# Products on half tiles, products of zeros in early gaps, and a new order of three half groups, in an attention kernel with two gated layers

## The chip, the cores and the metric

The kernel runs on one core of a Trainium2 chip. The time is the device time of one execution in microseconds (us), and a kernel is judged by the median of its runs. Engines are named as the profile names them: PE is TensorE (matrix products), DVE is VectorE, ACT is ScalarE, POOL is GpSimd, SP issues the DMA transfers. PEld is the loading of weights into PE.

## What is computed

Eight heads of linear attention with a decaying state run over four batches of 768 tokens. The 3072 tokens then go through two gated layers.

```python
# attention: B=4, H=8, S=768, D=48
for t in range(S):
    state = alpha[:, :, t, :, None] * state + einsum('bhd,bhe->bhde', k[:, :, t], v[:, :, t])
    y[:, :, t] = einsum('bhd,bhde->bhe', q[:, :, t], state)
x = y.transpose(0, 2, 1, 3).reshape(3072, 384)
# layer one: d_ff = 2048
h = x @ w_in;  x = (h * cos(h)) @ w_out
# layer two: d_ff = 1536
out = ((x @ w_a) * (x @ w_b)) @ w_out2
```

## The kernel before

**Units.** Attention is done in 48 units. A unit is 64 tokens of one batch with all 8 heads (12 units to a batch). For a unit DVE scans the decays forward (L303) and backward (L315), with a reciprocal between them (L312). `m` holds queries times forward decay and is made on POOL by two instructions of 48 partitions (L327). `k` holds keys times backward decay (L340, on DVE for units 0 to 7, on POOL after that). PE then forms the scores (L374) and the transposed keys (L383). DVE masks the scores (L407 in units 0 to 15, four instructions at L413 later), and ACT copies the keys (L389). PE next forms the new part of the state (L444, old state L450) and the outputs (L461). Units 0 to 15 have a separate product of the old state with `m` (L466, in the units that have an old state). It takes the state as one operand of 112 rows, half of which meet zeros in `m`, and each of its eight products stands behind an output product. From unit 16 on the state lies beside the values and needs no product of its own. ACT (L505) and DVE (L508) write each output as a high and a low part into the input tile `x_t` of the layers. DVE brings the state to the next unit (L535), from unit 16 on by two sums (L546) and two POOL instructions (L549).

From unit 8 on, one "block" on PE holds the outputs of a unit, the scores and transposed keys of the next unit and the new state of this one.

**Groups and steps.** 8 units (512 tokens) are a group; there are 6. Layer one is done in 96 steps (g, f): group g with slice f of the 16 slices of d_ff. A step has 9 products of 512 columns into a bank `hp` (L656), then round, fraction, sine, product and the split into two parts (ACT L706, DVE L709, ACT L714, DVE L717, ACT L721, DVE L725), then 9 products into the accumulator `acc_t` (L663). I call 9 such products a "PE group" of work. Layer two has 72 steps of 27 products (L656 and L663 again).

**Weights.** Layer one's weights arrive in 16 pairs, each 768 KB (L595). A pair is converted by ACT (L599, L604), by DVE (L610, L616), by ACT (L625) and by POOL (L636). A pair is needed from the first step of its f on.

**What sets the order.** The code does not emit instructions directly. It enters operations with an estimated duration and due time into a `Plan`, which lists them by its own rules, and each engine then runs its instructions in the listed order. `h_at` holds the due times of the steps, here group after group; `unit_due` holds those of the units. The 8 units of group 1 are due along the 16 steps of group 0, 1.7 steps apart, and so on. The order of the steps is this loop:

```python
    for g in range(NG):
        for f in range(NF1):
            h_at.append(t)
            t += TAU0 if g == 0 else TAU if g < NG - 1 else TAUL
```

**Products of zeros.** `keep_warm` issues products of zeros into accumulator bank 0 (L671): 15 at the start, one behind each of units 0 to 7. Their results are not used.

Of the kernel before, what the change touches and what calls it, by code (L numbers as in the profile page):

```python
# [57 lines left out]
NLATE = NPAIR2 - NPAIR1  # L58
DVE_DECAY = 0
ACT_LOW = 16  # L60
FIRST_UNIT, EVERY = 0.6, 1.7
PE, DVE, ACT, POOL, SP = range(5)


class Plan:
# [39 lines left out]
    def run(self):  # L105
# [56 lines left out]
        self.done = done  # L162
        return done
# [3 lines left out]
def chunked(ctx: ExitStack, tc: tile.TileContext, u_in: bass.AP, wts: bass.AP, out: bass.AP, in_range: bass.AP):  # L167
# [3 lines left out]
    xpool = ctx.enter_context(tc.tile_pool(name="xpool", bufs=2))  # L171
# [50 lines left out]
    h_at = []  # L222
    t = T0
    for g in range(NG):
        for f in range(NF1):
            h_at.append(t)
            t += TAU0 if g == 0 else TAU if g < NG - 1 else TAUL
# [39 lines left out]

    def xtile(g):
        if g not in xg:
            t = xpool.tile([P, 2, NP, G], F32R, name="x_t")  # L270
            xg[g] = t[:, 0], t[:, 1], t
        return xg[g]

    def plan_load(u):
        d, ops = un[u], U[u]
        if "ld" in ops:
            return ops["ld"]
        def load():
            if u < UG:
                t = wpool.tile([P, 2, 2 * DM], F32R, name="w_t").bitcast(F32)  # L280
                d["in"] = t.rearrange("p a c -> p (a c)")[:, 0:IN_COLS]
            else:
                d["in"] = att.tile([P, IN_COLS], F32, name="in_t", bufs=NIN)
            cols = W_A + 2 * NE4 if u < APART else IN_COLS
            cuts = (0, NA + 1, cols) if u == 0 else (0, cols)
            for c0, c1 in zip(cuts, cuts[1:]):
                nc.sync.dma_start(out=d["in"][:, c0:c1], in_=u_in[u, :, c0:c1])

        ops["ld"] = op(SP, 1.5, load, lag=1.7)
        ops["in_last"] = take("w_t", NPAIR1, ops["ld"]) if u < UG else take("in", NIN, ops["ld"])  # L290
        return ops["ld"]

    def plan_front(u):
# [20 lines left out]
        def scan_r():  # L314
# [13 lines left out]
                    m[rows, i + apart], part(u, 0)[rows], d["a"][rows, :, 1:], op=ALU.mult  # L328
# [3 lines left out]
            for rows, i in HEADS  # L332
# [29 lines left out]
    def plan_scores(u, block=None):  # L362
# [7 lines left out]
        def score():  # L370
            for c in range(2):
                for b in range(2):
                    for rows, h in HEADS:
                        nc.tensor.matmul(  # L374
                            sc_t[rows_of(b, h), b, c, :], kt[rows, 2 * b + c, :],
                            m[rows, h + apart, 2 * b + c, :], start=True, stop=True,
                        )
# [44 lines left out]
    def plan_back(u):  # L422
# [32 lines left out]
        def outputs():  # L455
            for p in range(NP):
                b, c = divmod(p, 2)
                for h, r0, n in ((0, 0, C), (1, 64, D)):
# [3 lines left out]
                        ys_t[r0:r0 + n, b, c, :], w[0:k_rows], m[0:k_rows, 0 if apart else h, p, :],  # L462
                        start=True, stop=not carry,
# [18 lines left out]
        else:  # L482
# [11 lines left out]
            us = ou = op(PE, 1.75 + (1.0 if carry else 0.0), block, [kn, ld, *mk, *ma, *before], due=due)  # L494
# [19 lines left out]
        if off == 0:  # L514
            E["xl", g] = take("x", 2, xh)
            E["xfirst", g] = xh
# [152 lines left out]
    def keep_warm(n):  # L669
        for _ in range(n):  # L670
            nc.tensor.matmul(warm[0:64, :], zeros[:, 0:64], zeros, start=True, stop=True)  # L671


    x2, x2s = {}, {}

    def plan_step(g, f):
        s = H[1, g, f] = {}
        i = g * NF1 + f
        at = h_at[i]
# [59 lines left out]
        def mm2():  # L739
            if f == 0:  # L740
                acc[g] = [acc_t[:, j] for j in range(KT)]
            into(acc[g], w1s[f, 1], s["hi"], s["lo"], f == 0, f == NF1 - 1)

        o = op(PE, 2.05, mm2, [gh, gl, H[1, g, f - 1]["o"] if f else None], due=at + 11.0)
        if g == 0 and f == 0:
            need(o, *(x for u in range(UG) for x in U[u]["read"]))
        if f == 0:
# [5 lines left out]
        if f == NF1 - 1:  # L753
            def evac(j):
                if j == 0:
                    x2[g] = (right[0] if g < NG - 2 else late[0]).tile([P, KT, G], F32, name=f"x2_{g}")
                nc.scalar.mul(x2[g][:, j, :], acc[g][j], TWO_PI / WS)

            gate = E["right"] if g < NG - 2 else E["late"]
            ev, e0 = [], None  # L760
            for j in range(KT):
                e0 = op(ACT, 0.6, lambda j=j: evac(j), [o, gate, e0])
# [5 lines left out]
    def plan_x2(g):  # L768
# [4 lines left out]
        for j in range(KT):  # L773
            def hi(j=j):
                if j == 0:
                    t = xpool.tile([P, 2, NP, G], F32R, name="x_t")
# [9 lines left out]
            if j == 0:  # L786
                E["x2l", g] = take("x", 2, h)
# [88 lines left out]
    with tc.manual_schedule():  # L876
# [44 lines left out]
        for g in range(NG):  # L921
            for f in range(NF1):
                plan_step(g, f)
# [11 lines left out]
def step_by_step(  # L935
# [76 lines left out]
    with tc.For_i(0, NG, 1) as g:  # L1012
        cols = bass.ds(g * G, G)
        x = pool.tile([P, KT, G], F32, name="g_x", bufs=1)
        for j in range(KT):
            for r0, f0, n in (
                (0, 2 * j * D, D), (48, 6 * D + j, 16), (64, (2 * j + 1) * D, D), (112, 7 * D + j, 16)
# [118 lines left out]
```

## Time and profile before

| what | us |
|---|---|
| runs of the kernel | 973.31, 973.96, 976.26 (median 973.96) |
| the profiled execution's own time | 973.26 |
| its span, first to last instruction | 971.4 |
| PE busy in the span | 939.9 (97%) |
| DVE, ACT, POOL busy | 540.5, 403.2, 226.5 |

The profile takes one execution. A busy PE is not PE at its peak: its matmuls overlap, and small products that wait on each other also count. Shares over the whole span mix stages with different limits, so the stages have to be read apart. The granted clock of PE (PEclk) is 1.00 at 2.4 GHz and 0.50 at 1.2 GHz; its mean over the span is 0.991.

### The profile page before, as it was taken

What the parts mean: (1) busy time and instruction counts of PE and PEld (TensorE: products, weight loads), DVE (VectorE), ACT (ScalarE), POOL (GpSimd) and SP (SyncE); (2) the same over time, 40 slices, a digit from 0 to 9 for tenths busy, and PEclk for the clock granted to TensorE, in tenths of its full rate; (3) what the DMA queues carried; (4) which work ended last, traced back from release to release, by engine and by line L of the source; (5) the groups of instructions that cost most, each with busy time, mean ns of one, the idle gap of its engine ahead of it and who ended that gap; (6) DMA issues with size and microseconds to landing.
All of it is one profiled execution on the core that took longest, in us unless ns stands there. A gap on an engine that the chain in (4) does not pass through costs nothing.

```text
span 971.4 us, 16849 instructions
## 1 busy us (share of the span) xinstructions
PE 939.9 (97%) x6935; PEld 766.3 (79%) x6935; DVE 540.5 (56%) x951; ACT 403.2 (42%) x754; POOL 226.5 (23%) x259
## 2 busy tenths in 40 slices
PE   6798989999999999999999999999999999999996
PEld 4677768888888888888887888888888888888884
DVE  7899998767777786776777842222222222222221
ACT  3477755545545455446665523112113113112111
POOL 4556543313322232312224321001001001000000
PEclk8999999999999999999999999999999999999998
DMA  9355412212221221203223400000000000000000
GB/s 369 106 199 184 164 38 78 90 62 81 88 63 54 89 89 54 64 1 139 98 98 112 149 0 33 1 1 33 1 0 33 1 1 33 0 1 33 1 1 36
DMA packets 17700, 64.96 MB, mean 67 GB/s; under 512 B 2384, under 2 KB 4816, under 8 KB 17616
## 3 DMA queue, kind: packets, MB, share of 16 engines
q1 hardware_dynamic: 17616, 63.81, 19.0%
q8 instruction: 56, 0.92, 0.4%
q14 instruction: 28, 0.23, 0.1%
HBM read 56.72 MB, written 4.72 MB: 63 GB/s over the span
## 4 chain that ended last, share of the span: by engine, by line
PE 87%; DVE 6%; DMA 2%; ACT 2%; issue 1%; POOL 1%; SPq 0%; ACTq 0%
PE acc_t L663 33%; PE hp L656 18%; PE xy L656 15%; PE ap L656 15%; PE xy L461 2%; DMA st_t<-wts 2%; PE xy L374 1%; DVE wf_t L610 1%; DVE wf_t L616 1%; DMA w_t<-u_in 1%; PE xy L383 1%; DVE c_t L709 1%; DVE ar_t L303 1%; PE xy L444 1%; DVE glo_t L725 1%
## 5 line engine op out<-in xcount | busy, mean ns | idle before, releaser
L663 PE MATMUL acc_t<-ghi_t,w_t 128*128 128x512 f32 x972 | 301.1, 391 | 1.0 <-ACT ghi_t L721 1.0
L656 PE MATMUL hp<-x_t,w_t 128*128 128x512 f32 (+1 forms) x882 | 216.4, 390 | 3.2 <-DMA x_t<-x_t 3.2
L663 PEld LDWEIGHTS acc_t<-ghi_t,w_t 128*128 128x128 f32 x972 | 181.6, 188 | 39.3 <-ACT ghi_t L721 1.9
L663 PE MATMUL acc_t<-glo_t,w_t 128*128 128x512 f32 x486 | 190.1, 391 | 3.8 <-DVE glo_t L725 3.8
L822 DVE TENSOR_TENSOR xy<-c_t,xy 128x512 f32<-128x512 f32 x72 | 50.1, 696 | 258.0 <-PE xy L656 257.9
L656 PEld LDWEIGHTS hp<-x_t,w_t 128*128 128x128 f32 x882 | 161.1, 188 | 36.8 <-ACT w_t L625 3.3
L656 PE MATMUL xy<-x_t,w_t 128*128 128x512 f32 x594 | 145.6, 390 | 0.0
L656 PE MATMUL ap<-x_t,w_t 128*128 128x512 f32 x540 | 132.2, 389 | 0.0
L656 PEld LDWEIGHTS xy<-x_t,w_t 128*128 128x128 f32 x594 | 111.5, 188 | 23.4
L656 PEld LDWEIGHTS ap<-x_t,w_t 128*128 128x128 f32 x540 | 101.4, 188 | 21.1
L819 ACT COPY c_t<-ap 128x512 f32<-128x512 f32 x72 | 42.3, 587 | 167.9 <-PE ap L656 167.8
L663 PEld LDWEIGHTS acc_t<-glo_t,w_t 128*128 128x128 f32 x486 | 91.2, 188 | 25.6 <-DVE glo_t L725 6.4
L826 ACT CAST ghi_t<-xy 128x512 fp32r<-128x512 f32 x72 | 42.2, 586 | 138.3 <-DVE xy L822 138.3
L706 ACT ACTIVATE c_t<-hp 128x512 int32<-128x512 f32 x96 | 57.5, 599 | 67.4 <-PE hp L656 67.1
L636 POOL TENSOR_TENSOR w_t<-wf_t,w_t 128x768 fp32r<-128x768 f32 x32 | 64.0, 1999 | 92.1 <-ACT w_t L625 92.1
L781 POOL TENSOR_TENSOR x_t<-x,x_t 128x512 fp32r<-128x512 f32 x18 | 23.7, 1343 | 251.0 <-ACT x_t L778 251.0
L714 ACT ACTIVATE c_t<-c_t 128x512 f32<-128x512 f32 x96 | 60.6, 631 | 46.7 <-DVE c_t L709 45.9
L709 DVE CUSTOM_DVE_ANT_0 c_t<-c_t,hp 128x512 f32<-128x512 int32 x96 | 65.6, 683 | 25.6 <-ACT c_t L706 24.7
L721 ACT CAST ghi_t<-hp 128x512 fp32r<-128x512 f32 x96 | 56.4, 587 | 54.1 <-DVE hp L717 53.5
L717 DVE TENSOR_TENSOR hp<-c_t,hp 128x512 f32<-128x512 f32 x96 | 65.8, 685 | 19.7 <-ACT c_t L714 19.2
L830 DVE TENSOR_TENSOR glo_t<-xy,ghi_t 128x512 fp32r<-128x512 f32 x72 | 49.8, 692 | 47.3 <-ACT ghi_t L826 47.3
L725 DVE TENSOR_TENSOR glo_t<-hp,ghi_t 128x512 fp32r<-128x512 f32 x96 | 65.7, 684 | 17.1 <-ACT ghi_t L721 16.3
(100 smaller groups left out, 923.3 us busy)
## 6 DMA issues: line engine op xcount, KB each, us to landing
st_t<-wts SPq DMA_DIRECT2D x34, 768.0 KB, 4.3
in_t<-u_in SPq DMA_DIRECT2D x32, 626.0 KB, 3.8
in_t<-u_in SPq DMA_DIRECT2D x8, 578.0 KB, 9.5
out<-o_t SPq DMA_DIRECT2D x18, 256.0 KB, 2.1
w_t<-u_in SPq DMA_DIRECT2D x7, 578.0 KB, 7.8
x_t<-x_t SPq DMA_DIRECT2D x48, 48.0 KB, 2.9
w_t<-u_in SPq DMA_DIRECT2D x1, 447.5 KB, 3.5
w_t<-u_in SPq DMA_DIRECT2D x1, 130.5 KB, 2.2
```

The costliest lines, as they stand in the source:

```text
L636: nc.gpsimd.tensor_tensor(t[:, 1], conv.pop(i), t[:, 0].bitcast(F32), op=ALU.subtract)
L656: nc.tensor.matmul(acc, wt[:, w, j * P:(j + 1) * P], r[:, j, :], start=i == 0, stop=i == len(terms) - 1)
L663: nc.tensor.matmul(accs[j], wt[:, w, j * P:(j + 1) * P], r, start=first and i == 0, stop=last and i == 2)
L706: nc.scalar.activation(s["c"].bitcast(I32), s["u"], AF.Identity, bias=-0.25, scale=-1.0)
L709: nc.vector._custom_dve(TENSOR_ADD_SAT, out=s["c"], in0=s["c"].bitcast(I32), in1=s["u"], s0=0.25, s1=-0.75)
L714: nc.scalar.activation(s["c"], s["c"], AF.Sin, bias=math.pi / 2, scale=TWO_PI)
L717: nc.vector.tensor_tensor(s["u"], s["c"], s["u"], op=ALU.mult)
L721: nc.scalar.copy(s["hi"], s["u"])
L725: nc.vector.tensor_tensor(s["lo"], s["u"], s["hi"].bitcast(F32), op=ALU.subtract)
L819: nc.scalar.copy(s["c"], s["a"])
L822: nc.vector.tensor_tensor(s["b"], s["c"], s["b"], op=ALU.mult)
L830: nc.vector.tensor_tensor(s["lo"], s["b"], s["hi"].bitcast(F32), op=ALU.subtract)
```

## The change

Three things are changed, with what they need.

1. The product of the old state works on 48 rows instead of 112. `m` of units 0 to 15 loses its zero half (two planes instead of three), its two POOL instructions become one of 112 partitions, and the eight state products of a unit stand together behind its output products. The heads of two of the four pairs swap their rows in the output, so the list of rows in the weights changes (`LOW`, `HIGH`). The loads of units 0 to 15 get 16 more columns.
2. The one product of zeros behind each of units 0 to 7 goes. In its place `filled` puts products of zeros wherever the plan sees a gap on PE before its 75th microsecond: 40 beside the 15 at the start. When the accumulator is in use they add zeros to it.
3. Layer one runs steps (0, 0..7), then (1, 0..15), then (0, 8..15), then groups 2 to 5. The accumulator of the first half of group 0 is copied out by ACT, and DVE adds the second half to it (three instructions). Units 8 to 15 are due 0.9 of a step apart along the first 8 steps. Units 16 to 23 are due 0.85 of a step apart from step 24 on, because their `x` tile is that of group 1 (`SLOT`). Layer one's first `x` tiles and `x2` of group 0 get fixed places.

```diff
+LOW, HIGH = (0, 2, 5, 7), (1, 3, 4, 6)
+F0 = 8
+STEPS = (
+    [(0, f) for f in range(F0)] + [(1, f) for f in range(NF1)] + [(0, f) for f in range(F0, NF1)]
+    + [(g, f) for g in range(2, NG) for f in range(NF1)]
+)
+SLOT = (0, 1, 1, 0, 1, 0), (1, 0, 1, 0, 1, 0)
...
-        return done
+        return self.filled(done)
+
+    WARM, WARM_UNTIL, WARM_GAP = 0.39, 75.0, 0.35
+
+    def filled(self, done):
+
+        out, end = [], None
+        for o in done:
+            if o["engine"] == PE:
+                if end is not None and o["start"] < self.WARM_UNTIL:
+                    n = int((o["start"] - end - self.WARM_GAP) / self.WARM)
+                    if n > 0:
+                        out.append(dict(o, i=-1, us=n * self.WARM, start=end, fn=lambda n=n: self.warm(n)))
+                end = o["start"] + o["us"]
+            out.append(o)
+        return out
...
-    m_t = [att.tile([P, 3, NP, C], F32, name=f"m{i}", bufs=1) for i in range(3)]
-    for i, t in enumerate(m_t):
-        (nc.gpsimd if i else nc.vector).memset(t[:, 1:3], 0.0)
+    m_t = [att.tile([P, 2, NP, C], F32, name=f"m{i}", bufs=1) for i in range(3)]
...
+        t += TAU0 if n < F0 else TAUL if n < F0 + NF1 or g == NG - 1 else TAU
...
-        i, part = divmod((u // UG - 1) * NF1 + FIRST_UNIT + EVERY * (u % UG), 1)
+        g, n = divmod(u, UG)
+        first, every = {1: (0.0, 0.9), 2: (F0 + NF1 + 0.3, 0.85)}.get(g, ((g - 1) * NF1 + FIRST_UNIT, EVERY))
+        i, part = divmod(first + every * n, 1)
...
-            for rows, i in HEADS
+            for rows, i in (((slice(0, 112), 1),) if apart else HEADS)
...
-                    if carry:
-                        nc.tensor.matmul(
-                            ys_t[r0:r0 + D, b, c, :], s_t[u % 2][:, p * D:p * D + D], m[0:112, h + 1, p, :],
-                            start=False, stop=True,
-                        )
-            if u < UG:
-                keep_warm(1)
+            if carry:
+                for c in range(2):
+                    for b in range(2):
+                        for rows, h in HEADS:
+                            p, r0 = 2 * b + c, rows_of(b, h).start
+                            nc.tensor.matmul(
+                                ys_t[r0:r0 + D, b, c, :], s_t[u % 2][rows, p * D:p * D + D], m[rows, 1, p, :],
+                                start=False, stop=c == 1,
+                            )
...
-        if f == NF1 - 1:
+        if ends:
...
+                if g == 0 and f == NF1 - 1:
+                    nc.vector.scalar_tensor_tensor(
+                        x2[g][:, j, :], acc[g][j], TWO_PI / WS, x2[g][:, j, :], op0=ALU.mult, op1=ALU.add
+                    )
+                else:
+                    nc.scalar.mul(x2[g][:, j, :], acc[g][j], TWO_PI / WS)
...
-        for g in range(NG):
-            for f in range(NF1):
-                plan_step(g, f)
+        for g, f in STEPS:
+            plan_step(g, f)
```

The order of instructions that the plan makes of this is seen at three places. In the changed file lines are numbered anew: L486 is the output product (before L461), L495 the state product (L466), L467 and L473 the new and old state (L444, L450), L397 and L406 scores and transposed keys (L374, L383), L698 zeros (L671), L683 and L690 the layers' products (L656, L663). On DVE L326 and L338 are the scans (L303, L315), L335 the reciprocal (L312), L637 and L643 the weights' bits (L610, L616), L430 the mask (L407), L562 the state (L535), L535 the output's low part (L508), L739, L747 and L755 a step's fraction, product and low part (L709, L717, L725).

PE, unit 2 at the end of its new state, before:

```order
L450 MATMUL xy<-s_105,ident 112x96 x2
L461 MATMUL xy<-m_101,w_t 64x64
L466 MATMUL xy<-m_101,s_105 48x64
L461 MATMUL xy<-m_101,w_t 48x64
L466 MATMUL xy<-m_101,s_105 48x64
```

Three more such fours follow, then one product of zeros. The same place after the change:

```order
L473 MATMUL xy<-s_102,ident 112x96 x2
L486 MATMUL xy<-m_101,w_t 64x64
L486 MATMUL xy<-m_101,w_t 48x64
L486 MATMUL xy<-m_101,w_t 64x64
L486 MATMUL xy<-m_101,w_t 48x64 x2
L486 MATMUL xy<-m_101,w_t 64x64
L486 MATMUL xy<-m_101,w_t 48x64
L486 MATMUL xy<-m_101,w_t 64x64
L495 MATMUL xy<-m_101,s_102 48x64 x8
L397 MATMUL acc_t<-m_99,k_105 64x64 x8
L406 MATMUL acc_t<-ident,k_105 64x48 x8
```

The state products moved behind the outputs, and the zeros moved behind the next unit's transposed keys.

DVE, from the first step's low part to the second step's product, before (`m_99` is here the mask of unit 9; unit 10's comes later):

```order
L315 SCALAR_TENSOR_TENSOR ar_t<-in_t,last 112x260
L725 TENSOR_TENSOR glo_t<-hp,ghi_t 128x512
L610 SCALAR_TENSOR_TENSOR wf_t<-wf_t,st_t 128x768
L535 TENSOR_TENSOR s_106<-xy,ar_t 112x192
L407 TENSOR_TENSOR m_99<-xy,mask 128x256
L508 SCALAR_TENSOR_TENSOR x_t<-xy,x_t 112x4x64
L709 ISA c_t<-c_t,hp 128x512
L616 SCALAR_TENSOR_TENSOR wf_t<-st_t,wf_t 128x768
L717 TENSOR_TENSOR hp<-c_t,hp 128x512
L303 SCALAR_TENSOR_TENSOR ar_t<-in_t,first 112x260
L610 SCALAR_TENSOR_TENSOR wf_t<-wf_t,st_t 128x768
```

And after, from the first step's fraction to the second's:

```order
L739 ISA c_t<-c_t,hp 128x512
L338 SCALAR_TENSOR_TENSOR ar_t<-in_t,last 112x260
L562 TENSOR_TENSOR s_103<-xy,ar_t 112x192
L430 TENSOR_TENSOR m_99<-xy,mask 128x256
L535 SCALAR_TENSOR_TENSOR x_119<-xy,x_119 112x4x64
L747 TENSOR_TENSOR hp<-c_t,hp 128x512
L637 SCALAR_TENSOR_TENSOR wf_t<-wf_t,st_t 128x768
L643 SCALAR_TENSOR_TENSOR wf_t<-st_t,wf_t 128x768
L755 TENSOR_TENSOR glo_t<-hp,ghi_t 128x512
L326 SCALAR_TENSOR_TENSOR ar_t<-in_t,first 112x260
L562 TENSOR_TENSOR s_102<-xy,ar_t 112x192
L430 TENSOR_TENSOR m_100<-xy,mask 128x256
```

The units of group 1 moved forward: unit 10's mask (to `m_100`) now stands ahead of the second step's fraction. Counted over the whole list ahead of the 16th step's fraction, DVE has 20 forward scans, 19 backward scans and 16 weight pairs before, and 18, 18 and 15 after; the masks of units 0 to 15 and 15 earlier steps are ahead of it in both.

PE, steps 24 and 25 after the change, with the blocks of units 17 and 18:

```order
L486 MATMUL xy<-m_101,in_t 64x64
L397 MATMUL xy<-m_99,k_104 64x64 x8
L406 MATMUL xy<-ident,k_104 64x48 x8
L467 MATMUL xy<-in_t,kn_107 48x48 x8
L683 MATMUL hp<-x_118,w_t 128x512 x9
L690 MATMUL acc_t<-ghi_t,w_t 128x512 x2
L690 MATMUL acc_t<-glo_t,w_t 128x512
L690 MATMUL acc_t<-ghi_t,w_t 128x512 x2
L690 MATMUL acc_t<-glo_t,w_t 128x512
L690 MATMUL acc_t<-ghi_t,w_t 128x512 x2
L690 MATMUL acc_t<-glo_t,w_t 128x512
L486 MATMUL xy<-m_99,in_t 64x64
```

Two or three PE groups stand between blocks there, two in all cases but one, through units 16 to 23; before, two to four stood between the same units, four in most cases. No block stands between unit 15's and unit 16's, and unit 16's comes behind the first products of step (1, 15).

## Rows read from the trace of the kernel before

**Rows 1.** Windows: length, busy us of PE, PEld, DVE, ACT, POOL; clock, DMA, GB/s.

```profile
12.60:19.43 6.83, 5.04 (x85) 4.12 (x85) 3.57 (x10) 1.30 (x3) 2.98 (x4) 0.50 1.03 419
...
37.60:125.00 87.40, 76.79 (x951) 62.08 (x944) 82.00 (x117) 63.20 (x115) 54.91 (x42) 0.98 0.50 171
125.00:139.00 14.00, 12.88 (x56) 10.03 (x55) 13.72 (x25) 6.49 (x12) 5.98 (x7) 1.00 0.06 16
139.00:450.00 311.00, 311.00 (x3070) 252.19 (x3069) 231.49 (x496) 158.25 (x328) 90.56 (x149) 1.00 0.22 72
450.00:962.00 512.00, 511.71 (x2250) 421.74 (x2248) 185.44 (x254) 158.09 (x262) 58.45 (x35) 1.00 0.09 31
```

**Rows 2.** Timeline of PE in layer two: start, duration, instruction (PE groups).

```profile
898.52 2.21 PE L656 MATMUL ap<-x_t,w_t 128*128 128x512 f32 x9
900.56 2.20 PE L656 MATMUL xy<-x_t,w_t 128*128 128x512 f32 x9
```

**Rows 3.** Timeline of PE: units 1 and 2, from new state to next scores.

```profile
14.30 0.68 PE L444 MATMUL acc_t<-w_t,kn 64*48 64x48 f32 x16 [2.27 <-DVE m L407]
...
18.23 0.70 PE L374 MATMUL xy<-m,k 48*64 48x64 f32 x16
...
20.57 0.45 PE L444 MATMUL xy<-w_t,kn 64*48 64x48 f32 x16 [1.23 <-DVE m L407]
...
22.79 0.46 PE L374 MATMUL acc_t<-m,k 48*64 48x64 f32 x16
```

**Rows 4.** Timeline of DVE: masks of units 1 and 7.

```profile
13.86 0.39 DVE L407 TENSOR_TENSOR m<-acc_t,mask 128x256 f32<-128x256 f32 x1
...
38.16 0.42 DVE L407 TENSOR_TENSOR m<-acc_t,mask 128x256 f32<-128x256 f32 x1 [0.42 <-ACT kn L389]
```

**Rows 5.** Timeline at 52 us: POOL and a DVE instruction on weights.

```profile
52.67 0.68 POOL L327 TENSOR_TENSOR m<-in_t,ar_t 48x256 f32<-48x256 f32 x1
52.71 3.28 DVE L610 SCALAR_TENSOR_TENSOR wf_t<-wf_t,st_t 128x768 int32<-128x768 int32 x1
...
53.31 1.86 POOL L636 TENSOR_TENSOR w_t<-wf_t,w_t 128x768 fp32r<-128x768 f32 x1
```

**Rows 6.** Groups by form, 37.6 to 125 us: count, busy us, mean ns, idle before.

```profile
L327 POOL TENSOR_TENSOR m<-in_t,ar_t 48x256 f32<-48x256 f32 x18 | 17.6, 977 | 4.0 <-DVE ar_t L303 3.2
...
L610 DVE SCALAR_TENSOR_TENSOR wf_t<-wf_t,st_t 128x768 int32<-128x768 int32 x14 | 20.0, 1429 | 0.1
L616 DVE SCALAR_TENSOR_TENSOR wf_t<-st_t,wf_t 128x768 int32<-128x768 int32 x14 | 16.3, 1165 | 0.0
L303 DVE TENSOR_TENSOR_SCAN ar_t<-in_t,first 112x260 f32<-112x260 f32 x9 | 11.7, 1301 | 0.0
```

**Rows 7.** Timeline: DVE's and POOL's instructions when they are not held up.

```profile
43.05 0.93 DVE L616 SCALAR_TENSOR_TENSOR wf_t<-st_t,wf_t 128x768 int32<-128x768 int32 x1
...
52.02 0.69 POOL L340 TENSOR_TENSOR k<-ar_t,in_t 112x256 f32<-112x256 f32 x1 [2.35 <-DVE ar_t L315]
```

**Rows 8.** Groups of DVE by form, 139 to 214 us (columns as in rows 6).

```profile
L709 DVE CUSTOM_DVE_ANT_0 c_t<-c_t,hp 128x512 f32<-128x512 int32 x16 | 10.9, 682 | 2.0 <-ACT c_t L706 1.6
...
L413 DVE TENSOR_TENSOR m<-xy,mask 64x128 f32<-64x128 f32 x32 | 9.1, 285 | 0.4
...
L303 DVE TENSOR_TENSOR_SCAN ar_t<-in_t,first 112x260 f32<-112x260 f32 x8 | 5.8, 731 | 5.3 <-DMA in_t<-u_in 5.2
L546 DVE TENSOR_TENSOR sm_t<-xy,in_t 48x192 f32<-48x192 f32 x14 | 5.0, 354 | 3.6 <-ACT x_t L505 3.4
```

**Rows 9.** Timeline of a block and what follows it.

```profile
201.69 0.68 PE L461 MATMUL xy<-m,in_t 112*64 112x64 f32 x16
...
202.91 2.35 PE L656 MATMUL hp<-x_t,w_t 128*128 128x512 f32 x9
...
203.76 0.39 ACT L505 ACTIVATE x_t<-xy 112x256 fp32r<-112x256 f32 x1
...
204.50 0.41 DVE L508 SCALAR_TENSOR_TENSOR x_t<-xy,x_t 112x256 fp32r<-112x256 f32 x1
```

More of the change, by code (lines that the diff above doesn't have):

```diff
@@ L266, in carried @@
         return tuple((rows, vs(u, i)[rows]) for rows, i in HEADS)
+    x_t = [xpool.tile([P, 2, NP, G], F32R, name=f"x{i}") for i in range(2)]
+    for g in range(NG):
+        t = x_t[SLOT[0][g]]
+        xg[g] = t[:, 0], t[:, 1], t
     def xtile(g):
-        if g not in xg:
-            t = xpool.tile([P, 2, NP, G], F32R, name="x_t")
-            xg[g] = t[:, 0], t[:, 1], t
         return xg[g]
@@ L327, in plan_front @@
                 lambda rows=rows, i=i: nc.gpsimd.tensor_tensor(
-                    m[rows, i + apart], part(u, 0)[rows], d["a"][rows, :, 1:], op=ALU.mult
+                    m[rows, i], part(u, 0)[rows], d["a"][rows, :, 1:], op=ALU.mult
                 ),
@@ L375, in score @@
                             sc_t[rows_of(b, h), b, c, :], kt[rows, 2 * b + c, :],
-                            m[rows, h + apart, 2 * b + c, :], start=True, stop=True,
+                            m[rows, 1 if apart else h, 2 * b + c, :], start=True, stop=True,
                         )
@@ L457, in outputs @@
                 b, c = divmod(p, 2)
-                for h, r0, n in ((0, 0, C), (1, 64, D)):
+                for h in range(2):
+                    rows = rows_of(b, h)
+                    n = D if rows.start else C
                     w = d["in"][:, W_A + h * NE4 + p * D:W_A + h * NE4 + p * D + n]
@@ L492, in block @@
                     old_state()
-            us = ou = op(PE, 1.75 + (1.0 if carry else 0.0), block, [kn, ld, *mk, *ma, *before], due=due)
+            us = ou = op(PE, 1.5 + (0.85 if carry else 0.0), block, [kn, ld, *mk, *ma, *before], due=due)
         ops["us_op"] = [us]
@@ L514, in plan_back @@
         if off == 0:
-            E["xl", g] = take("x", 2, xh)
+            E["xl", g] = take(f"x{SLOT[0][g]}", 1, xh)
             E["xfirst", g] = xh
@@ L670, in keep_warm @@
         for _ in range(n):
-            nc.tensor.matmul(warm[0:64, :], zeros[:, 0:64], zeros, start=True, stop=True)
-    x2, x2s = {}, {}
+            nc.tensor.matmul(warm[0:64, :], zeros[:, 0:64], zeros, start=0 not in acc, stop=0 not in acc)
+    plan.warm = keep_warm
+    x2, x2s = {0: small.tile([P, KT, G], F32, name="x2_0")}, {}
     def plan_step(g, f):
         s = H[1, g, f] = {}
-        i = g * NF1 + f
-        at = h_at[i]
+        at = h_at[h_of[g, f]]
+        begins = f == 0 or (g == 0 and f == F0)
+        ends = f == NF1 - 1 or (g == 0 and f == F0 - 1)
         def mm():
@@ L739, in mm2 @@
         def mm2():
[L740 to L744, printed above, removed]
+            acc[g] = [acc_t[:, j] for j in range(KT)]
+            into(acc[g], w1s[f, 1], s["hi"], s["lo"], begins, ends)
+        o = op(PE, 2.05, mm2, [gh, gl, None if begins else H[1, g, f - 1]["o"]], due=at + 11.0)
         if g == 0 and f == 0:
             need(o, *(x for u in range(UG) for x in U[u]["read"]))
-        if f == 0:
+        if begins:
             E["acc", g] = [take(f"acc{j}", 1, o) for j in range(KT)]
```

34 lines of the change are left out of this document (16 added, 18 removed).

## Prediction

> **What bounds the kernel now.** I read the page's totals first, then windows by stage. From 139 us on PE is busy without a gap, 311.0 of 311 us and 511.7 of 512 us [rows 1]. There a PE group follows the last by 2.04 us (900.56 less 898.52) [rows 2]. That part is bound by PE's fixed work, and the change leaves that work as it is. What the change can win lies before 139 us: how early PE has work that it can do without gaps, and how much of it is done by then. There PE is not the bound. From 37.6 to 125 us it is busy 76.8 of 87.4 us, while DVE is busy 82.0 us (94%), and from 125 to 139 us DVE is busy 13.7 of 14 us [rows 1]. The reader is to see in these rows that the engine that sets the pace changes at about 139 us, and that a us saved on DVE before it moves everything behind it.
>
> Three things make the early part long. First, the clock: from 12.60 to 19.43 us PE was granted 0.50, the level of 1.2 GHz [rows 1], after a stretch with few products. Unit 1's work on PE, from its new state to the next scores, takes 3.93 us there (18.23 less 14.30); unit 2's, at 2.4 GHz, takes 2.22 us (22.79 less 20.57) [rows 3]. Second, the chain from unit to unit: the masks of units 1 and 7 are 24.3 us apart [rows 4], 4.05 us a unit. Third, DVE is held up by POOL. At 52.71 us a DVE instruction on weights begins just after POOL's `m` and lasts 3.28 us, until POOL's next instruction has ended too, at 55.17 us (53.31 and 1.86) [rows 5]; left alone, the like of it takes 0.93 us [rows 7]. From 37.6 to 125 us L610 has a mean of 1.43 us, L616 of 1.17 and L303 of 1.30 [rows 6], against 0.93 [rows 7] and 0.73 [rows 8]. That is 14 x 0.50 and 14 x 0.24 and 9 x 0.57, together 15.5 us of DVE's 82.0 us spent on waiting while it counts as busy.
>
> **The change part by part.**
>
> *Startup.* The zeros stand in PE's waits (two of them between a unit's transposed keys and its new state), where before only one stood behind each unit. If they keep the clock at 2.4 GHz, unit 1 gains 1.7 us [rows 3]. `m` needs one POOL instruction instead of two; a POOL instruction of 112 partitions and 256 columns takes 0.69 us [rows 7], as much as one of 48 partitions, 0.68 us [rows 5], so each unit has `m` 0.7 us sooner. Between unit 1's mask and unit 7's I expect 3.5 us a unit for 4.05, since a shorter POOL step and a shorter wait for DVE lie on the chain of a part of the units only: 6 x 0.55 is 3.3 us, the clock's gain in it. Against this, DVE's list now has the first weight pair behind more of the units' work. Bounds: 0 (units are paced by DVE's order anyway) and 6.3 us (3.0 us a unit). I take 3.3.
>
> *POOL from 37.6 us on.* Units 8 to 15 lose one `m` instruction each: 8 x 0.68 is 5.5 us less that DVE can be held up by. By how much do DVE's 15.5 us of waiting shrink? POOL is busy 54.9 us there [rows 1], so in proportion 15.5 x 5.5 / 54.9 is 1.6 us; if each was waited for in full, 5.5 us. Rows 5 show `m` at the head of such a wait, which speaks for more than the proportion. I take 3.
>
> What stands behind these waits, the Trainium skill says in "SBUF — State Buffer", section "SBUF: two separate sides": the port pair that VectorE and GpSimd share is an exclusive lock, held for a whole instruction by whichever starts first, while the other blocks. This trace agrees that it blocks, but here the wait of 3.28 us went through two POOL instructions, not one, so the row decides. By that rule, with one instruction waited for at a time, the term would be the 1.6, and the sum 5.4 and 968.4.
>
> *The new order of steps.* Ahead of the 16th step's fraction DVE has, by the counts of its list, two forward scans and one backward scan less and one weight pair less: 3 x 0.73 and 2 x 0.93 is 4.1 us [rows 7, 8]. All else ahead of it is the same. So the same number of steps is ready 4.1 us sooner, if DVE stays the bound to there. By then PE's needs are met: 32 PE groups are 65 us, and eight blocks with state products are, as an estimate, at most twice the 1.22 us of a block without (202.91 less 201.69), 20 us, in some 95 us [rows 2, 9]. Bounds: 0 and 4.1; I take 4. That eight pairs are enough for the first 16 steps matters less than it seems, since the units of group 1, moved forward, take DVE's time in their place.
>
> *What the new order costs.* Units 16 to 23 now stand within 8 steps (24 to 31). PE's work there is 16 x 2.04 and 8 x 1.22 [rows 2, 9], 42.4 us. DVE's is 8 steps of 3 x 0.68, eight units of 4 x 0.285, 2 x 0.354 and 0.41, and, by its list, six scan pairs of 2 x 0.73 [rows 8, 9]: 16.3, 18.1 and 8.8, together 43.2 us, without a wait for POOL. So there DVE is as loaded as PE. The chain from block to block must fit into 1.22 and two PE groups, 5.3 us: the block's start to ACT's output is 2.07 us (203.76 less 201.69), that takes 0.39, and DVE then needs 0.41, 4 x 0.285 and 2 x 0.354 us, 4.7 us in all [rows 8, 9]. It fits by 0.6 us, if nothing else stands between on DVE. In the trace of before DVE's masks of such a unit stand between a step's instructions, and there are four PE groups to cover it. Bounds: 0 and 16 us (2 us at each of eight blocks, one step's DVE work of 2.04 us in the way); I take 3.
>
> *The rest.* Copying out the accumulator once more is three ACT copies and three DVE sums, at most 3 x 0.69 us; it is hidden by the two PE groups (4.08 us) that the lists place behind each handover, else it costs 2 us. The state products in 64-row tiles cost PE less (outputs alone last 0.68 us in rows 9), but PE waits in that stage, so nothing. The zeros behind the first 37 us stand where the plan sees a gap; if PE isn't idle there, some 15 of them cost 0.23 us each (a ninth of 2.04) [rows 2], 3 us. I take 0.5. The memsets that go lie ahead of the first load's landing: nothing.
>
> *Sum.* 3.3 and 3 and 4, less 3 and 0.5, is 6.8 us. The profiled execution takes 973.3 us (its span of 971.4 and 1.9 around it), and would come to 966.5; the median of the runs is 0.7 us higher, so I predict 967.
>
> **Rivals.**
> *Little comes of it* (20%). DVE and POOL have nearly the same work to do up to the 16th step, so only the 4.1 us of order and part of the wait come off, and the dense stage takes them back: 4 and 1 less 3 is 2 us, 972. For it: DVE at 94% in the old order too. Against it: the clock's 1.7 us and 4.05 us a unit in startup, where DVE is not full.
> *Slower by the dense stage* (11%). Each of the blocks of units 16 to 23 waits for its masks or its state behind a step's DVE instructions. The place is steps 24 to 31; the price is up to 16 us against a gain of 9.8, so it decides from 1.2 us a block on; at 2 us it gives 980.
> *All gaps close* (14%). PE idles 10.6 us from 37.6 to 125 and 1.1 us to 139 [rows 1]. If the new order fills these 11.7 us, where I count 7, and startup brings 6.3 with no cost later, the gain is 18 us: 956.
> *The zeros fail to hold the clock.* "TensorE: Matmul & The Clock Gate" of the Trainium skill, section "What's actually happening", says that the throttled state is the default and activity releases it; no run here shows yet that zeros suffice between units. Without the clock's 1.7 us the sum by rows is 5.1 and the time 969: this lies inside the likeliest case.
>
> **How the numbers follow.** The likeliest case (55%) is a gain of 3.5 to 12 us, 962 to 970.5, with 967 from the sum. Little is 20%, slower 11%, all gaps 14%. The measurement tells 0.3%, 2.9 us, from no change. Faster than 971.0 us: the likeliest, all gaps, and a fifth of little, 0.73; within 2.9 us of the old time: 0.15; slower: the dense stage and a small tail, 0.12. The range takes in most of all gaps and of little, from 957 to 975, and leaves out the slower case and the far end of the other, 2 in 10.
>
> **What would show it.** Right: PE's clock 1.00 from about 6 us to the end; masks of units 1 and 7 some 21 us apart; L610's and L303's means in the stage of the first 8 steps below 1.4 and 1.3 us; PE without gaps by about 128 us, ten us sooner; one or two us lost in the blocks of steps 24 to 31. Wrong: a clock of 0.50 in startup; PE waiting for L436 or the state between the blocks of units 16 to 23, by more than 1.2 us each; or DVE below 90% in the first 8 steps with PE idle too, which would mean that waits along the chain of units, not DVE's load, set the pace.

## The result and the profile after

The changed kernel takes 964.95 us (median of 20 runs, 963.21 to 974.48), the kernel before beside it 974.56 us (20 runs, 972.42 to 978.97). The ratio of the two sets of runs is 0.9914, with an interval of 0.9895 to 0.9933: 8.4 us faster (the medians alone differ by 9.6). 15 of the 20 runs lie between 963.2 and 966.3 us, with a mean granted clock of 0.994 to 0.998; one took 970.2 at 0.988, and four 973.8 to 974.5 at 0.980 to 0.982. The execution that was profiled is one of these four, so its rows show the order of work rightly, and the time of the early stage at its worst. No execution of the 15 was profiled.

Its windows, with the columns and stretches of [rows 1], and two more:

```profile
12.60:19.43 6.83, 5.28 (x170) 4.39 (x170) 4.42 (x11) 2.65 (x6) 1.36 (x2) 1.00 1.02 418
22.10:56.20 34.10, 30.86 (x433) 22.35 (x433) 18.74 (x40) 12.42 (x27) 8.16 (x9) 0.50 0.24 84
37.60:125.00 87.40, 83.28 (x1016) 64.89 (x1017) 74.84 (x127) 60.98 (x113) 41.80 (x34) 0.89 0.50 173
125.00:139.00 14.00, 14.00 (x64) 11.58 (x63) 11.77 (x16) 12.65 (x21) 5.81 (x4) 1.00 0.16 58
139.00:450.00 311.00, 310.58 (x3067) 251.68 (x3066) 238.31 (x503) 155.37 (x324) 94.18 (x150) 1.00 0.21 67
450.00:962.00 512.00, 511.76 (x2251) 422.05 (x2250) 185.83 (x254) 159.77 (x263) 59.74 (x36) 1.00 0.09 34
...
185.00:225.00 40.00, 39.58 (x487) 31.63 (x486) 35.20 (x86) 20.31 (x48) 18.18 (x30) 1.00 0.38 124
```

At 12.60 us the clock is no longer at 0.50, but from 22.10 us on it is, for 34.1 us. From 37.6 to 125 us PE is busy 83.28 us for 76.79 [rows 1], up to 56.20 us at half clock, and from 125 to 139 us it has no gap. Later it loses 0.42 us, in the stage of steps 24 to 31 (178 to 222 us): from 185 to 225 us PE is busy 39.58 of 40 us beside a DVE that is busy 35.20.

The groups by form from 37.6 to 125 us, as in [rows 6]; L326, L637 and L643 were L303, L610 and L616:

```profile
L637 DVE SCALAR_TENSOR_TENSOR wf_t<-wf_t,st_t 128x768 int32<-128x768 int32 x13 | 13.9, 1069 | 0.0
L643 DVE SCALAR_TENSOR_TENSOR wf_t<-st_t,wf_t 128x768 int32<-128x768 int32 x12 | 12.2, 1014 | 0.2
...
L326 DVE TENSOR_TENSOR_SCAN ar_t<-in_t,first 112x260 f32<-112x260 f32 x10 | 8.5, 847 | 0.0
```

DVE's waiting for POOL, worked out as in the prediction, is 13 x 0.14 and 12 x 0.08 and 10 x 0.12, 4.0 us where it was 15.5.

Where the time went, by the starts of the same pieces of work in four traces (PE groups are counted from the first layer product; "33rd" has 32 groups, 16 steps, behind it, "65th" has 64 groups, 32 steps):

| us | before | changed | changed, third profile | zeros in a free bank |
|---|---|---|---|---|
| mask of unit 7 | 38.2 | 41.5 | 41.1 | 35.8 |
| first layer product | 37.6 | 52.1 | 47.8 | 41.1 |
| 33rd group | 142.8 | 142.1 | 137.3 | 131.9 |
| 65th group | 221.0 | 222.3 | 217.9 | 212.4 |
| end of the span | 971.4 | 972.7 | 968.4 | 961.8 |
| the execution's own time | 973.3 | 974.5 | 970.1 | 963.7 |

The starts of unit 7's mask stand in these rows of DVE, for the changed kernel, its third profile, a_zeros_hp (zeros in a free bank) and a_old_order (the changed kernel with the old order of steps, see below):

```profile
41.48 0.42 DVE L430 TENSOR_TENSOR m<-acc_t,mask 128x256 f32<-128x256 f32 x1 [0.45 <-ACT kn L412]
41.06 0.42 DVE L430 TENSOR_TENSOR m<-acc_t,mask 128x256 f32<-128x256 f32 x1
35.81 0.42 DVE L430 TENSOR_TENSOR m<-acc_t,mask 128x256 f32<-128x256 f32 x1
34.64 0.42 DVE L425 TENSOR_TENSOR m<-acc_t,mask 128x256 f32<-128x256 f32 x1
```

The first layer product is not at the same place in the order: before, the first half of its group stands ahead of unit 7's new state and the second half, at 45.7 us, behind unit 8's transposed keys; after, both halves stand behind those keys. So its start alone says little, and unit 7's mask is the better mark of how startup went. From that mask to the 65th group the four take 182.9, 180.8, 176.9 and 176.6 us. The first 32 groups take 105.2 us before, with 11.7 us of idle time on PE, and 90.0, 89.5 and 90.8 after, with 2.0, 2.9 and 2.8 us of it; in part they are shorter because more of the units' work now lies ahead of them. The next 32 groups take 78.2 us before, and 80.2 to 80.6 after, with 64 small products of units more among them and 0.4 to 0.9 us of idle time, all of it in steps 24 to 31.

### The profile page after: what moved, and what is told of

It reads as the page before. It is cut to its first block, busy times and chain, and to the rows that moved or that the text cites. A ratio compares the mean times of both kernels' runs of the same rounds, so it can differ in the third digit from the quotient of the medians.

```text
span 972.7 us, 16931 instructions
## 1 busy us (share of the span) xinstructions
PE 952.6 (98%) x6967; PEld 772.6 (79%) x6967; DVE 534.0 (55%) x953; ACT 404.8 (42%) x754; POOL 208.9 (21%) x241
## 4 chain that ended last, share of the span: by engine, by line
PE 92%; DVE 2%; ACT 1%; DMA 1%; issue 0%; SPq 0%; POOL 0%; ACTq 0%; POOLq 0%; DVEq 0%
PE acc_t L690 34%; PE hp L683 20%; PE xy L683 15%; PE ap L683 15%; PE xy L486 2%; PE xy L397 1%; PE acc_t L698 1%; PE xy L467 1%; PE xy L406 1%; DMA st_t<-wts 1%; PE xy L473 0%; PE acc_t L486 0%; DMA x<-x 0%; ACT x L532 0%; PE xy L495 0%
## 5 line engine op out<-in xcount | busy, mean ns | idle before, releaser
L690 PE MATMUL acc_t<-ghi_t,w_t 128*128 128x512 f32 x972 | 300.9, 391 | 0.0
L683 PE MATMUL hp<-x,w_t 128*128 128x512 f32 (+1 forms) x882 | 217.2, 392 | 1.5 <-DMA x<-x 1.2
L690 PEld LDWEIGHTS acc_t<-ghi_t,w_t 128*128 128x128 f32 x972 | 181.5, 188 | 38.2 <-issue 0.2
L683 PEld LDWEIGHTS hp<-x,w_t 128*128 128x128 f32 x882 | 162.4, 190 | 37.0 <-ACT c_t L744 1.6
L690 PE MATMUL acc_t<-glo_t,w_t 128*128 128x512 f32 x486 | 189.6, 390 | 0.5 <-DVE glo_t L755 0.4
L683 PE MATMUL xy<-x,w_t 128*128 128x512 f32 x594 | 145.6, 389 | 0.0
L683 PE MATMUL ap<-x,w_t 128*128 128x512 f32 x540 | 132.2, 389 | 0.0
L683 PEld LDWEIGHTS xy<-x,w_t 128*128 128x128 f32 x594 | 111.5, 188 | 23.5
L683 PEld LDWEIGHTS ap<-x,w_t 128*128 128x128 f32 x540 | 101.4, 188 | 21.2
L854 ACT COPY c_t<-ap 128x512 f32<-128x512 f32 x72 | 42.3, 587 | 169.5 <-PE ap L683 169.4
L690 PEld LDWEIGHTS acc_t<-glo_t,w_t 128*128 128x128 f32 x486 | 91.2, 188 | 20.6 <-DVE glo_t L755 1.3
L861 ACT CAST ghi_t<-xy 128x512 fp32r<-128x512 f32 x72 | 42.3, 587 | 140.7 <-DVE xy L857 140.7
L663 POOL TENSOR_TENSOR w_t<-wf_t,w_t 128x768 fp32r<-128x768 f32 x32 | 64.7, 2023 | 96.7 <-ACT w_t L652 96.5
L739 DVE CUSTOM_DVE_ANT_0 c_t<-c_t,hp 128x512 f32<-128x512 int32 x96 | 65.4, 682 | 25.0 <-ACT c_t L736 24.4
L816 POOL TENSOR_TENSOR x<-x,x 128x512 fp32r<-128x512 f32 x18 | 23.7, 1345 | 250.3 <-ACT x L813 160.0
L747 DVE TENSOR_TENSOR hp<-c_t,hp 128x512 f32<-128x512 f32 x96 | 65.8, 685 | 19.3 <-ACT c_t L744 19.3
L755 DVE TENSOR_TENSOR glo_t<-hp,ghi_t 128x512 fp32r<-128x512 f32 x96 | 65.6, 683 | 18.8 <-ACT ghi_t L751 18.3
```

The costliest lines, as they stand in the source:

```text
L663: nc.gpsimd.tensor_tensor(t[:, 1], conv.pop(i), t[:, 0].bitcast(F32), op=ALU.subtract)
L683: nc.tensor.matmul(acc, wt[:, w, j * P:(j + 1) * P], r[:, j, :], start=i == 0, stop=i == len(terms) - 1)
L690: nc.tensor.matmul(accs[j], wt[:, w, j * P:(j + 1) * P], r, start=first and i == 0, stop=last and i == 2)
L739: nc.vector._custom_dve(TENSOR_ADD_SAT, out=s["c"], in0=s["c"].bitcast(I32), in1=s["u"], s0=0.25, s1=-0.75)
L747: nc.vector.tensor_tensor(s["u"], s["c"], s["u"], op=ALU.mult)
L755: nc.vector.tensor_tensor(s["lo"], s["u"], s["hi"].bitcast(F32), op=ALU.subtract)
```

## Experiments

**The three parts, apart and in pairs.** The change has three parts: half tiles (with one POOL instruction for `m`), zeros placed by the plan, and the new order. Theory: the gain comes from POOL's shorter part and from the order, and the zeros save the clock. Rival: one of them carries it all.

```diff
 a_old_order: the changed kernel with the old order
-STEPS = (
...
+STEPS = [(g, f) for g in range(NG) for f in range(NF1)]
 a_zeros_as_before: the changed kernel without zeros by the plan
-        return self.filled(done)
+        return done
...
+            if u < UG:
+                keep_warm(1)
 b_half_tiles: both of these edits
 a_whole_tiles: the changed kernel with m, scores and outputs as before
-            for rows, i in (((slice(0, 112), 1),) if apart else HEADS)
+            for rows, i in HEADS
 b_new_order: a_whole_tiles, with zeros as before
```

These are the main lines of each edit; the due times of the units and the slots of `x` go with the order, and the planes of `m` with the tiles. In the last two the zeros are read from another tile that is zero there (112 rows for 128), for space. The eighth kernel, the plan's zeros alone, was not run.

> Half tiles and the plan's products of zeros, with the steps group after group as before. By the prediction's terms: 3.3 and 3 less 0.5, 5.8 us less than before, near 969, in executions where the clock holds. The rival that the order brings nearly all: 1 to 2 us less than before.

> Half tiles and one POOL instruction for m alone; order of steps and products of zeros as before. By the prediction's terms: POOL 3 us and the half of the startup term that is not the clock's, 1.6 us, together 4.6 us less than before, near 970. The rival that the order of steps brings nearly all of it: within 1 us of before.

> The new order of steps alone, with whole tiles, two POOL instructions for m and one product of zeros behind each of units 0 to 7 (the zeros are read from another tile, for space). By the prediction's terms: 4 us gained and 3 lost in steps 24 to 31, 1 us less than before, near 973.5. The rival that the order brings nearly all: 6 us or more less than before.

> The changed kernel with whole tiles again: state products on 112 rows beside each output product, two POOL instructions for m; new order and the plan's zeros kept. Theory: half tiles are what makes PE's work in startup too thin to hold the clock, so this one holds it in every execution; the time is that of the changed kernel's faster executions plus up to 3 us for POOL, 964 to 967 without a second level. Rival: half tiles matter for POOL alone, and the two levels stay.

> The changed kernel without the plan's zeros: 15 at the start and one behind each of units 0 to 7, as before; half tiles and new order kept. Theory: without them the half tiles let the clock fall for some 60 us, as in the run of half tiles alone, and the time is 975 to 985. By the prediction's own terms it would be 1.7 less 0.5, 1.2 us, above the changed kernel, 966.

| kernel | half tiles | zeros by plan | new order | median us | ratio to before | clock of its runs |
|---|---|---|---|---|---|---|
| before | | | | 974.56 | 1 | 0.979 to 0.992 |
| b_half_tiles | x | | | 987.29 | 1.0063 to 1.0129 | 0.963 to 0.978 |
| b_new_order | | | x | 972.02 | 0.9940 to 0.9972 | 0.987 to 0.993 |
| a_old_order | x | x | | 970.81 | 0.9945 to 0.9988 | 0.980 to 0.996 |
| a_zeros_as_before | x | | x | 976.03 | 0.9986 to 1.0026 | 0.969 to 0.989 |
| a_whole_tiles | | x | x | 976.66 | 0.9996 to 1.0028 | 0.985 to 0.995 |
| changed | x | x | x | 964.95 | 0.9895 to 0.9933 | 0.980 to 0.998 |

Each ratio is to the runs of the kernel before beside it, whose medians were 974.56 to 975.57 us; the clocks of the first row are those of its runs beside the experiments. Of the five expectations two came near, 969 for a_old_order and 973.5 for b_new_order. The 975 to 985 us of a_zeros_as_before hold in its median, and not in five of its runs (968.59 to 973.76). Half tiles alone were to win and lost, and a_whole_tiles was to lie at 964 to 967 us with the clock held, and did neither.

The parts don't add up. By medians half tiles alone make the kernel 12.7 us slower; with the other two in place they are worth 11.7 us (976.66 less 964.95). The zeros are worth 16.5 us with half tiles in the old order (987.29 less 970.81) and 11.1 in the new, and cost 4.6 us without half tiles (976.66 less 972.02). Only the order gains in every pair that was run: 2.5 us alone, 5.9 with the rest, 11.3 beside half tiles without the zeros (987.29 less 976.03).

The clock is one link, for what the zeros give with half tiles: at about the same mean clock a_zeros_as_before took 968.59 us (its run at 0.989) and the changed kernel 970.22 (0.988), so there the zeros bring the clock and nothing beside it, as far as one run of each can tell. It does not explain a_whole_tiles: its four runs at 0.993 to 0.995 took 974.59 to 976.80 us, ten more than the changed kernel at such a clock. Two rows of b_half_tiles show the fall, all engines and clock from 6 us on (columns of [rows 1]):

```profile
6.00:10.00 4.00, 2.13 (x52) 1.23 (x51) 2.60 (x6) 0.92 (x3) 0.69 (x1) 0.98 1.02 418
10.00:14.00 4.00, 3.10 (x73) 2.36 (x69) 1.89 (x5) 1.44 (x4) 0.68 (x1) 0.50 1.03 420
```

The clock fell to 0.50 at 9.9 us, after PE had been busy 2.13 of the 4 us ahead, and in this execution it stayed there for 61.4 us. In the profile of a_old_order, with the plan's zeros, PE was busy 3.96 us from 6 to 10 us and the clock did not fall there. That the zeros do this is not shown by these two alone: a_zeros_as_before has the 23 zeros of b_half_tiles, and in its profile, taken of the fastest of its twelve runs, PE was busy 2.58 us there and the clock fell only at 30.2 us.

**One POOL instruction or two.** The edit splits `m` again and keeps the half tiles.

```diff
-            for rows, i in (((slice(0, 112), 1),) if apart else HEADS)
+            for rows, i in (((slice(64, 112), 1), (slice(0, 64), 1)) if apart else HEADS)
```

> The changed kernel with two POOL instructions for m in units 0 to 15 again (64 and 48 partitions of the same plane), half tiles on PE kept. This measures the prediction's POOL term by itself: 3 us more (0 to 5.5) from 37.6 us on, and some 1.6 us in startup, 968 to 969. Rival: POOL is not waited for once the units stand in their new order, and the time is that of the changed kernel within 1 us.

It took 981.18 us (973.92 to 987.50; ratio 1.0029 to 1.0089) and so lies far above both the expectation and its rival. Its clock varied (0.972 to 0.994), so only its three runs at 0.993 and more are compared: 973.9, 975.0 and 977.3 us, where the changed kernel's runs at 0.994 and 0.995 took 963.97 to 966.30. That is about 9 us. In its trace the first 32 groups take 95.3 us (46.9 to 142.2), 5.8 more than in the third profile of the changed kernel, and unit 1's mask starts at 14.7 us for 11.5. The plan also lists the work anew for the longer POOL part: 60 zeros for 55, 31 of them ahead of unit 1's scores for 25, and unit 0's mask at 10.7 us for 8.9. So this is the price of the second instruction with what the plan makes of it. POOL's rows for unit 1's `m` show the instructions themselves, two that last 1.71 us together in a_two_m, one of 0.68 in the changed kernel:

```profile
7.99 1.71 POOL L350 TENSOR_TENSOR m<-w_t,ar_t 48x256 f32<-48x256 f32 x2 [1.34 <-DVE ar_t L326]
```

```profile
7.49 0.68 POOL L350 TENSOR_TENSOR m<-w_t,ar_t 112x256 f32<-112x256 f32 x1 [1.19 <-DVE ar_t L326]
```

So the one instruction is the larger part of what "half tiles" are worth; since a_whole_tiles took as long at such a clock (974.59 to 976.80 us), the half tiles on PE show no gain of their own.

**More zeros, and where they stand.** The plan counts a zero as 0.39 us and leaves 0.35 us of a gap free; with 0.2 and 0.2 there are 109 zeros for 55.

> The changed kernel with about twice the products of zeros (109 for 55) in the same gaps. Theory: the two levels of time, near 964 and near 974, come from one event, a clock of 0.50 for some 30 us from about 21 us on, which PE's thin work there lets happen. Then with more zeros no execution lies near 974, all near 963 at a mean clock of 0.995 or more, and the median drops by 1 to 2 us. Rival: the zeros stand in the way of PE's own work, 54 x 0.23 is 12 us at most, and the time rises by several us in all executions.

The clock was held, 0.997 or 0.998 in each of the nine runs, as the theory had it, but the time was 972.23 us (971.18 to 973.35), several us more in all of them, as the rival had it. PE in the changed kernel shows why (timeline: start, duration, instruction, idle time and its releaser):

```profile
11.95 0.59 PE L698 MATMUL acc_t<-zeros 128*64 128x512 bf16 x2 [0.90 <-DVE m L430]
12.47 0.45 PE L467 MATMUL acc_t<-w_t,kn 64*48 64x48 f32 x16
...
15.36 0.59 PE L698 MATMUL acc_t<-zeros 128*64 128x512 bf16 x2 [0.44 <-DVE s L562]
15.88 0.45 PE L467 MATMUL xy<-w_t,kn 64*48 64x48 f32 x16
...
20.43 0.81 PE L698 MATMUL acc_t<-zeros 128*64 128x512 bf16 x3 [2.11 <-DVE m L430]
```

The zeros do not fill the wait. PE idles first, is released by DVE's mask or state, then runs the zeros, and the unit's state products stand behind them. The zeros write a bank of `acc_t`, the tile in which the odd units' scores and states lie too, so a batch waits for DVE's work on that tile.

So three kernels write the zeros to a bank of the ring `hp`, until that ring's third step:

```diff
 a_zeros_hp
-        warm = acc_t[:, 0]
+        warm = bank("warm", "hp", 3)
...
-        for _ in range(n):
+        for _ in range(0 if "u" in H.get((1, 0, 2), {}) else n):
 a_more_zeros_hp: and
-    WARM, WARM_UNTIL, WARM_GAP = 0.39, 75.0, 0.35
+    WARM, WARM_UNTIL, WARM_GAP = 0.2, 75.0, 0.2
 a_late_zeros_hp: a_zeros_hp, with 0.26 and 0.2 from 13 us of the plan on
```

> The changed kernel with its products of zeros written to a bank that no other engine reads (one of the ring of layer products, until the ring's third step) in place of a bank of acc_t, which the odd units' scores and states share. In the changed kernel a batch of zeros is itself released by VectorE's work on acc_t, so that it runs after the wait and ahead of the unit's state products (a batch of 2 at 11.95 us, released by the mask). Theory 1 (the zeros' place in the path costs time): each batch now runs inside the wait, the first layer product starts 2 to 5 us earlier than 52 us, and the time is 956 to 963 us. Theory 2 (the position of the zeros doesn't matter, PE's 0.25 us each are small change): 963 to 967 us, as the changed kernel.

> As the run before, with 104 zeros for 54 (a zero counted at 0.2 us for 0.39 us, and 0.2 us of the wait left free for 0.35). With 109 zeros in the shared bank the clock was held (0.997 to 0.998 in every execution) and the time was 972.2 us. Theory 1: the loss there was the zeros behind the waits; here they fill the waits, the clock is held in every execution, and the time is 954 to 962 us. Theory 2 (a batch that is longer than its wait holds up the unit whatever bank it writes): 966 to 973 us.

> The changed kernel with its zeros in a bank that no other engine reads, the 25 zeros ahead of unit 0's state products as in the changed kernel, and more behind them: 71 zeros in all for 54, mostly 3 a unit for 2. With 104 zeros and 11 more of them ahead of unit 0's state products the clock was held in every execution, but unit 1's mask stood at 14.9 us for 11.6, and the kernel took 967.15 us for 962.53. Theory 1 (what was lost there are the zeros ahead of unit 0 and those beyond the waits, about 0.25 us each): mask of unit 1 at 11.5 to 12 us, unit 7 at 34 to 36.5, the clock at 0.995 or more in every execution, 960 to 963 us. Theory 2 (any zero more in units 1 to 7 costs its 0.25 us a unit): 963.5 to 966 us at a held clock.

| kernel | zeros | median us | ratio to before | clock of its runs |
|---|---|---|---|---|
| a_zeros_hp | 54 | 962.53 (961.79 to 963.67, 4 runs) | 0.9838 to 0.9885 | 0.992 to 0.997 |
| a_late_zeros_hp | 71 | 963.89 (962.19 to 966.95, 5 runs) | 0.9860 to 0.9900 | 0.991 to 0.998 |
| a_more_zeros_hp | 104 | 967.15 (965.94 to 968.85, 6 runs) | 0.9895 to 0.9934 | 0.995 to 0.998 |

PE in a_zeros_hp, the same units:

```profile
11.12 0.62 PE L698 MATMUL warm<-zeros 128*64 128x512 bf16 x2
12.09 0.45 PE L467 MATMUL acc_t<-w_t,kn 64*48 64x48 f32 x16 [0.35 <-DVE m L430]
...
18.12 0.83 PE L698 MATMUL warm<-zeros 128*64 128x512 bf16 x3
20.59 0.45 PE L467 MATMUL acc_t<-w_t,kn 64*48 64x48 f32 x16 [1.63 <-DVE m L430]
```

Now the zeros run first and the wait that is left is shorter. The first layer product starts 11.0 us earlier than in the changed kernel's first profile (41.1 for 52.1), where 2 to 5 were expected, and the time lies in the range of theory 1, with one run of four just above it. At about the same clock and count, a_more_zeros_hp is 5.1 us faster than a_more_zeros (967.15 for 972.23): that is the price of standing behind the wait. a_zeros_hp is the fastest kernel here. Its median lies 2.4 us below the changed kernel's, though its slowest run (963.67) is no faster than the other's best (963.21); without a side by side of many runs I claim no more than that. More zeros gained nothing on top, as theory 2 of the run with 104 has it: with 104, unit 0's state products start at 12.85 us for 9.52, behind 11 more zeros, and the first layer product at 45.0 us for 41.1. With 71 the time is unclear against 54, and one run still lost the clock for 10.2 us, so neither theory of that run held in full.

**Two more profiles of the changed kernel.**

> The changed kernel once more, unaltered, for a profile. In 20 runs it came out near 964 us at a mean clock of 0.995 to 0.998, or near 974 us at 0.98. If the clock in the first 60 us is what parts the two, this profile shows either no stretch of 0.50 before 100 us and a span near 962, or such a stretch of about 34 us and a span near 972; a span near 962 with the long stretch, or near 972 without, would refute it.

> The changed kernel once more, for a profile of an execution whose clock isn't lowered for 30 us in the first 60 us. Theory: with the clock at half for less than 10 us after the first 10 us, the profiled execution takes 963 to 967 us, PE's group of step 33 (the 32nd behind the first) starts by 138 us, and the 65th by 218 us; the rival, that the clock there isn't what makes the difference between 964 and 974 us, wants 972 to 975 us at any clock.

They took 974.92 us at a clock of 0.983 and 970.13 at 0.989; the clock was at 0.50 for 30.7 us from 21.1 us on, and for 17.1 us from 21.2. So the first shows the long stretch and the long time together, one of the two outcomes that its theory allows, and the profile at a held clock that the second was to give was not had. But the order of times goes with the clock, with nothing else moved: from the 65th group to the end of the span they take 749.3 and 750.5 us, the first profile 750.5.

**The wait ahead of the fall.** In all three profiles of the changed kernel the clock falls at 21.1 to 22.1 us, behind one wait. ACT, DVE and the windows of the first of them:

```profile
18.21 0.89 ACT L626 ACTIVATE wf_t<-st_t 128x768 f32<-128x768 f32 x1 [2.87 <-DMA st_t<-wts]
...
19.63 0.30 ACT L412 COPY kn<-acc_t 128x192 f32<-128x192 f32 x1
```

```profile
19.96 0.42 DVE L430 TENSOR_TENSOR m<-acc_t,mask 128x256 f32<-128x256 f32 x1 [1.93 <-ACT kn L412]
```

```profile
18.00:22.00 4.00, 1.89 (x47) 1.29 (x39) 2.04 (x7) 2.99 (x7) 0.68 (x1) 1.00 1.02 413
22.00:26.00 4.00, 3.93 (x82) 2.88 (x83) 2.06 (x6) 2.13 (x6) 0.68 (x1) 0.51 0.93 378
```

ACT's first conversion of weights (L626) stands in its list ahead of unit 3's key copy (L412) and waits 2.87 us for its transfer; the copy's keys are needed by the mask, the mask by PE, and PE idles 2.11 us. Then the clock falls. The weights' conversion waits in the same place before the change (5.53 us, released at 18.62). That the wait makes the fall is argued from the order of events alone. Against it as a sure cause: a_old_order's profile has a PE wait of 1.81 us at the same place and its clock stayed at 1.00, and a_late_zeros_hp's has one of 0.83 us and its clock fell at 22.9. Entering that conversion behind unit 3's copy would have told; it was not tried.

## Why the prediction was right in the time and wrong in some steps

*Startup*, put at a gain of 3.3 us, came out at that size where the clock held, and as a loss where it didn't. In the three profiles of the changed kernel unit 7's mask starts at 41.5, 42.3 and 41.1 us for 38.2 [rows 4], 2.9 to 4.1 us later, and all three lost the clock behind unit 3. In the profile of a_old_order, which has the same units and zeros up to there, the clock stayed at 1.00 until 49.5 us, and the mask starts at 34.6, 3.5 us earlier than before. The way to it was another than forecast, so the size is in part luck: the masks of units 1 and 7 were to be some 21 us apart, and are 23.0 at full clock (a_old_order, a_more_zeros_hp), 24.2 with the zeros in a free bank and 30.0 in the first profile, for 24.3 before. The pace shortens by 0.2 us a unit at best, where 0.55 was put; the rest is unit 1's mask, 2.3 us earlier (11.6 for 13.9), which the sum had not counted.

The step that failed here is "the zeros stand in PE's waits". They stood behind them, which costs time (972.23 us for 967.15 with twice the zeros), and they did not hold the clock in every execution.

*The clock* was sized at 1.7 us, and a failure of the zeros at 969 us. The mechanism was named rightly, the size was not: the four runs that lost it took 974, ten us more than the rest. "TensorE: Matmul & The Clock Gate" of the Trainium skill, section "What's actually happening", has the throttled state as the default that activity releases; the rows agree in so far as PE with twice the zeros kept a mean clock of 0.997 or 0.998 in all nine runs of a_more_zeros.

*POOL from 37.6 us on*, put at 3, was about right. By the prediction's own count DVE's waiting in a_two_m is 6.8 us (13 x 0.05, 13 x 0.18 and 10 x 0.38), for 4.0 and 4.8 in the first and third profile of the changed kernel: one instruction saves 2.0 to 2.8 us of it. The first 32 groups take 5.8 us more there, but PE's idle time among them only 2.2 more (5.2 for 2.9); the rest is 38 small products more and 3.4 us at half clock from 61.9 us on. The 1.6 us of the proportion is below both. The prediction took the same 1.6 for the Trainium skill's rule of the lock ("SBUF — State Buffer", section "SBUF: two separate sides"), by which one instruction holds the shared ports and the other engine waits; that rule does not give the proportion by itself. What the prediction did not see is that DVE's waiting is not POOL's share alone: it shrank from 15.5 us to 5.4 with the old order (a_old_order) and to 6.5 with the order alone (b_new_order), where POOL still has its two instructions.

*The new order*, put at 4, and *its cost* in steps 24 to 31, put at 3, were to leave 1 us. From unit 7's mask to the 65th group the order alone saves 3.0 us (b_new_order), half tiles with the plan's zeros in the old order save 2.1 (a_old_order), and both together 6.0 (third profile). The cost was the term most wrongly sized: PE's idle time in steps 24 to 31 is 0.4 to 0.9 us in the four profiles, a tenth of a us for each of the eight blocks, so the margin of 0.6 us a block was enough but for that, and the rival that lived there falls.

An estimate for an execution that holds the clock, put together from two kernels since no such execution of the changed one was profiled, is 3.5 us of startup (a_old_order) and 6.0 from there on (third profile): 9.5 us, where the sum had 6.8. The 15 runs at 0.994 and more have a median of 964.1 us, 10.5 below the kernel before. The dense steps, put at 3, explain 2.1 to 2.6 us of what the sum lacks. The 8.4 us of all runs lies nearer to the 6.8 because the runs that lost the clock are in it, which the prediction had as a rival and not as a part of the same set of runs. So the time was hit in part by luck, by a cost put too high and a loss left out. "All gaps close" was the nearer of the rivals in its mechanism, PE's idle time in the first 32 groups fell from 11.7 us to 2.0 to 3.8 in the three profiles; but its 956 us was reached by no run. Of the signs, L637's and L326's means (1.07 and 0.85 us from 37.6 to 125 us) came true, and so did PE without gaps by 128 us; "a clock of 0.50 in startup", a sign of being wrong, came true as well.

## What to carry to other kernels

Filler work costs least if it can start when the wait starts: give it an output that no other engine reads, and look in the trace whether it runs ahead of the release or behind it. Work that is made cheaper on an engine that waits leaves it idler, and where the clock follows, that alone can cost more than the cheaper work saves; so measure such parts together. A sum of terms that comes out right is no proof of its terms: the starts of the same piece of work in both traces show which hold, and a "first" piece that has another place in the new order is not the same piece.

## What the runs showed of the hardware

At half clock PE is busy 30.86 of 34.10 us in the profile after and 3.93 of 4.00 just behind the fall, and the clock does not come back for that. Small products last longer there, as the outputs of units 2 and 3 show, ahead of the fall and behind it:

```profile
16.82 0.68 PE L486 MATMUL xy<-m,w_t 128*64 128x64 f32 x16
22.11 1.12 PE L486 MATMUL acc_t<-m,w_t 128*64 128x64 f32 x16
```

So a busy PE does not show that the clock is safe. The same kernel runs at 963 or at 974 us by what the clock does in its first 60 us (by the mean clock of its runs; where a profile shows the place, it lies there). The nine runs with 109 zeros, all at 0.997 or 0.998, were within 1.2 us of 972.2.
